# Rescheduling a fused attention and gated feed-forward kernel: eight heads per projection, background matmuls in every second slot, a pipelined prologue

## The chip, the cores and the metric

The kernel runs on one core of one Trainium2 chip. The metric is the device time of one execution in microseconds (us). Most executions of one kernel agree within 0.3% (the twelve of the old kernel lie between 1168.73 and 1172.42 us). Each run has a state; all comparisons here are between runs in the fast state, except where the text says otherwise. Engines are named as the profile names them: PE is TensorE (matmuls), PEld its weight loads, ACT is ScalarE, DVE is VectorE, POOL is GpSimd, SP is SyncE.

## The reference

The block has 2048 tokens of width 512, 32 heads of width 16 and a feed-forward width of 1792. All weights and inputs are bf16.

```python
def attention(x, wqkv, wo):                     # x: (1, 2048, 512)
    q, k, v = split_heads(x @ wqkv)             # 32 heads of 16
    p = softmax(q @ k.T * 16 ** -0.5)           # 2048 x 2048 for each head
    return merge_heads(p @ v) @ wo

def glu(x, w_gate, w_up, w_down):               # F = 1792
    return (sigmoid(x @ w_gate) * (x @ w_up)) @ w_down

h  = x + attention(layernorm(x), wqkv, wo)
h2 = h + glu(layernorm(h), w_gate, w_up, w_down)
```

The softmax needs 32 x 2048 x 2048 exponentials.

## The kernel before

The kernel has three parts: a prologue (layer norm, transposes, the first projections), a main loop over tiles of scores, and a tail (output projection and feed-forward of the last quarter of the queries).

One turn of the main loop handles three units of 128 keys x 512 queries of one head. I call a turn a **slot**. There are 683 of them, in four query chunks of about 171 slots. In a slot PE computes the next tile of scores (three row-tiled matmuls, K = 32), ACT computes one exponential over 1536 columns, and PE multiplies older exponentials with V (column-tiled matmuls, M = 17). Everything else (projections of later heads, output projection, feed-forward of the chunk before) is **background**: generators that advance by one step in every slot.

```python
    pss_next = scores(groups[0])
    for n, group in enumerate(groups):            # one slot
        pss = pss_next
        if n + 1 < len(groups):
            pss_next = scores(groups[n + 1])      # two score buffers
        pt = ptp.tile([P, GU, QC], BF16, name="pt")
        nc.scalar.activation(out=pt[:, 0:w, :], in_=pss[:, 0:w, :], func=ACT.Exp,
                             scale=DH ** -0.5)
        av(GU if len(avq) <= 2 * GU else 2 * GU)  # three value matmuls, or six
        ...
        step()                                    # one background step, mostly 4 matmuls
```

A projection handles four heads at a time, each padded with zeros from 16 to 32 rows so that it lands where the row-tiled scores want it. So half of each projection matmul multiplies zeros:

```python
    def proj_T(ps, w_pad, g, c, a=0, b=DC):
        for d in range(a, b):
            nc.tensor.matmul(ps[:], lhsT=w_pad[:, d, 4 * g:4 * g + 4, :].rearrange("p h r -> p (h r)"),
                             rhs=xnT[:, d, c * QC:(c + 1) * QC],
                             start=(d == 0), stop=(d == DC - 1))

    def prep_q(qc, g):                            # a background generator
        ps = pm_tile()                            # the only bank for the background
        proj_T(ps, wq_pad, g, qc)
        yield
        sq = q_evac(ps, qc, g)
        yield
        yield
        ps = pm_tile()
        q_shift_mm(ps, sq)                        # norms, for a bound on the scores
        yield
        q_shift(ps, qc, g)
```

The prologue does one chunk after the other, with all 16 tiles of V:

```python
    for c in range(NQC):
        chunk_ln(c)                  # statistics, normalise, transpose
        ...                          # padded weights, K of the first heads, Q of the first chunk
        for i in range(TQ):
            v_tile(bank0(), c * TQ + i, True)
    ...
    k4 = kmax_red(pk, 0)             # maxima, moved between partitions by four DMAs
```

## Time and profile before

The median is 1170.74 us. The profiled run is 1168.8 us long. First, the page's share of each engine, two rows of its table in 40 slices of the span (a digit is tenths busy; PEclk is the clock granted to PE; the clock records of this trace hold 1.0, printed as 9 and called full clock here, and 0.5, called half clock), and the chain that ended last:

```profile
PE 947.9 (81%) x5408; PEld 287.7 (25%) x5408; DVE 264.8 (23%) x526; ACT 981.0 (84%) x774; POOL 86.1 (7%) x82
...
ACT  2359889899987997999987997899988998999911
...
PEclk9778999776577998756678999765678998555589
...
ACT pt L471 37%; PE pm L147 6%; PE pss L403 6%; PE acc L431 5%; PE pm L352 4%; PE pss L502 2%; DVE hT L347 2%; PE pm L309 2%; PE b L201 2%; PE pm L336 1%; ACT th L340 1%; DVE xn L116 1%; DVE KT L156 1%; PE pm L344 1%; PE pss L511 1%
```

PE and ACT look equally busy, but matmul records overlap (at 448.46 us below, tiles of scores are recorded as 0.39 us long, and the value matmuls start 0.33 after them), so "81%" says little. The groups view (line, engine, operation, out<-in, count | busy us, mean ns | idle before it, and what ended that) says who waits for whom:

```profile
L471 ACT ACTIVATE pt<-pss 128x1536 bf16<-128x1536 f32 (+1 forms) x683 | 942.3, 1561 | 83.3 <-PE pss L403 61.0
L403 PE MATMUL pss<-qt,KT 32*128 32x512 bf16 x2048 | 337.2, 482 | 131.2 <-ACT pt L471 121.6
L147 PE MATMUL pm<-xnT,wq_pad 128*128 128x512 bf16 x124 | 50.4, 553 | 0.5 <-DVE sh L195 0.2
```

PE waits 121.6 us for ACT in front of the scores, so PE is not the bound on the whole; yet ACT waits 61.0 us for scores, so PE comes late at times. The padded Q projections take 553 ns in the mean, against 398 for the down projection (same shape), a first sign that they run at half clock (four of them hold PE for 1.82 us at half clock in this trace and for 0.96 at full). The mean of 1561 ns is not what one exponential costs: a record can start while the one before still runs (683 records of 1561 ns are 1066 us, but ACT was busy with them for 942.3). The ends of 520 of the 682 pairs of neighbouring exponentials lie 1.34 to 1.36 us apart, with a median of 1.344. So 683 of them need 918 us. A tanh between them (42 of them) is counted here with 0.44 us. The traces say 0.49: the intervals with a tanh in them are 1.834 us long in the median. What an interval has beyond 1.344 and 0.44 I call **loss**; it is worked out from the ends of the exponentials in the trace. So every loss below is about 2.1 us too high (42 x 0.05). The span then divides as follows.

| part of the span | us |
|---|---|
| until the first exponential starts | 73.7 |
| 683 exponentials x 1.344 | 918 |
| 42 tanh x 0.44 | 18.5 |
| loss: ACT late because PE was late | 100.1 |
| after the last exponential ends | 58.4 |

Where does the loss arise? The timeline (start us, duration, engine, line, what, count, and in brackets the idle time before it and what ended it) of a stretch at full clock, where a background step stands in each slot; weight loads are left out:

```profile
448.46 0.39 PE L403 MATMUL pss<-qt,KT 32*128 32x512 bf16 x3
448.79 0.39 PE L431 MATMUL acc<-pt,Vaug 128*17 128x512 bf16 x3
448.96 1.45 ACT L471 ACTIVATE pt<-pss 128x1536 bf16<-128x1536 f32 x1 [0.19 <-PE pss L403]
449.11 1.04 PE L352 MATMUL pm<-wd,hT 128*128 128x512 bf16 x4
450.08 0.39 PE L403 MATMUL pss<-qt,KT 32*128 32x512 bf16 x3
450.40 0.39 PE L431 MATMUL acc<-pt,Vaug 128*17 128x512 bf16 x3
450.57 1.45 ACT L471 ACTIVATE pt<-pss 128x1536 bf16<-128x1536 f32 x1 [0.16 <-PE pss L403]
```

From one tile of scores to the next PE needs 0.33 + 0.32 + 0.97 = 1.62 us, more than 1.344, so ACT idles 0.16 to 0.19 us before each exponential. A single full slot should be absorbed, since there are two score buffers (my reasoning); neighbouring full slots are not. Elsewhere a background step arrives at half clock:

```profile
532.24 0.61 PE L403 MATMUL pss<-qt,KT 32*128 32x512 bf16 x3 [0.20 <-ACT pt L471]
532.78 0.60 PE L431 MATMUL acc<-pt,Vaug 128*17 128x512 bf16 x3
533.58 0.61 PE L403 MATMUL pss<-qt,KT 32*128 32x512 bf16 x3 [0.20 <-ACT pt L471]
534.12 0.60 PE L431 MATMUL acc<-pt,Vaug 128*17 128x512 bf16 x1
534.65 1.79 PE L147 MATMUL pm<-xnT,wq_pad 128*128 128x512 bf16 x4
...
537.18 4.14 ACT L471 ACTIVATE pt<-pss 128x1536 bf16<-128x1536 f32 x3 [0.96 <-PE acc L431]
```

Slots without background work keep up at half clock (0.54 + 0.54 us < 1.344). But four full matmuls now take about 1.7 us, and ACT waits 0.96 us at once.

The background has one PSUM bank, and when the next background matmul has to wait until another engine has emptied the bank or made its operand, the scores that the program puts behind it on PE wait too.

The longest, 2.9 us, stand behind a finished group: DVE first works through four operations on the finished values (2.1 us) and only then empties the bank.

### The profile page before, as it was taken

The numbers are of one execution on the slowest core, as the hardware profiler recorded it, in microseconds if no ns is written. First come the engines' busy times: TensorE is split into PE (matmuls) and PEld (weight loads), VectorE is DVE, ScalarE is ACT, GpSimd is POOL, SyncE is SP. The second block draws the span as 40 slices with busy tenths as digits, with TensorE's granted clock in tenths as the row PEclk, the third lists the DMA queues.
The fourth block names the chain that finished last, engine by engine and source line by source line (L and its number), as shares of the span: only waits on it lengthen the run. The fifth ranks groups of instructions, "written<-read, shape, count | busy, mean of one in ns | idle before, by whom it ended". The sixth has DMA issues, their size and how long they took to land.

```text
span 1168.8 us, 13212 instructions
## 1 busy us (share of the span) xinstructions
PE 947.9 (81%) x5408; PEld 287.7 (25%) x5408; DVE 264.8 (23%) x526; ACT 981.0 (84%) x774; POOL 86.1 (7%) x82
## 2 busy tenths in 40 slices
PE   3668787878887988788887898788888988888878
PEld 1212222222222322222222232222222322222233
DVE  5423323311123211211123212211124211000063
ACT  2359889899987997999987997899988998999911
POOL 6022222200000000100000000100000000000000
PEclk9778999776577998756678999765678998555589
DMA  5000000050000000000000000000000001000000
GB/s 144 1 1 1 1 1 1 1 190 1 1 19 1 1 1 19 2 1 1 1 19 1 1 1 19 1 1 1 1 19 1 1 1 37 1 1 1 1 1 19
DMA packets 11741, 14.87 MB, mean 13 GB/s; under 512 B 928, under 2 KB 10528, under 8 KB 11680
## 3 DMA queue, kind: packets, MB, share of 16 engines
q1 hardware_dynamic: 9904, 11.93, 3.1%
q10 hardware_dynamic: 1584, 1.57, 0.4%
q0 software_dynamic: 192, 0.52, 0.3%
q8 instruction: 42, 0.69, 0.2%
q14 instruction: 19, 0.16, 0.0%
HBM read 11.80 MB, written 2.10 MB: 12 GB/s over the span
## 4 chain that ended last, share of the span: by engine, by line
ACT 39%; PE 33%; issue 15%; DVE 10%; DMA 1%; POOL 0%; SPq 0%; ACTq 0%; DVEq 0%; POOLq 0%
ACT pt L471 37%; PE pm L147 6%; PE pss L403 6%; PE acc L431 5%; PE pm L352 4%; PE pss L502 2%; DVE hT L347 2%; PE pm L309 2%; PE b L201 2%; PE pm L336 1%; ACT th L340 1%; DVE xn L116 1%; DVE KT L156 1%; PE pm L344 1%; PE pss L511 1%
## 5 line engine op out<-in xcount | busy, mean ns | idle before, releaser
L471 ACT ACTIVATE pt<-pss 128x1536 bf16<-128x1536 f32 (+1 forms) x683 | 942.3, 1561 | 83.3 <-PE pss L403 61.0
L403 PE MATMUL pss<-qt,KT 32*128 32x512 bf16 x2048 | 337.2, 482 | 131.2 <-ACT pt L471 121.6
L431 PE MATMUL acc<-pt,Vaug 128*17 128x512 bf16 x2048 | 340.2, 482 | 1.5 <-DVE xs L412 1.0
L403 PEld LDWEIGHTS <-KT 32*128 32x128 bf16 x2048 | 107.3, 94 | 410.4 <-issue 397.9
L431 PEld LDWEIGHTS <-Vaug 128*17 128x17 bf16 x2048 | 66.3, 89 | 222.9 <-issue 222.8
L412 DVE STREAM_TRANSPOSE xs<-acc 128x512 f32<-128x512 f32 x32 | 22.9, 717 | 430.5 <-PE acc L431 430.0
L161 POOL TENSOR_TENSOR sq<-qt 128x512 bf16<-128x512 bf16 x32 | 33.3, 1040 | 678.3 <-DVE qt L187 667.2
L347 DVE SCALAR_TENSOR_TENSOR hT<-th,pm 128x512 bf16<-128x512 f32 x42 | 28.8, 685 | 139.0 <-ACT pt L471 105.1
L336 PE MATMUL pm<-hnT,wg 128*128 128x512 bf16 x168 | 46.1, 399 | 10.8 <-DVE hT L347 10.8
L352 PE MATMUL pm<-wd,hT 128*128 128x512 bf16 x168 | 47.0, 398 | 9.4 <-DVE ob L362 8.6
L147 PE MATMUL pm<-xnT,wq_pad 128*128 128x512 bf16 x124 | 50.4, 553 | 0.5 <-DVE sh L195 0.2
L344 PE MATMUL pm<-hnT,wu 128*128 128x512 bf16 x168 | 44.1, 386 | 0.0
L340 ACT ACTIVATE th<-pm 128x512 f32<-128x512 f32 x42 | 32.9, 784 | 9.4 <-PE pm L336 9.4
L161 POOL TENSOR_TENSOR sq<-KT 128x512 bf16<-128x512 bf16 x32 | 33.3, 1040 | 99.7 <-DVE KT L156 57.6
L195 DVE TENSOR_SCALAR sh<-pm,kmax 4x512 bf16<-4x512 f32 x31 | 22.9, 738 | 67.3 <-PE acc L431 34.0
L505 ACT ACTIVATE th<-pss 128x512 f32<-128x512 f32 x14 | 8.4, 598 | 35.1 <-PE pss L502 35.1
L147 PE MATMUL pm<-xnT,wk_pad 128*128 128x512 bf16 x112 | 32.4, 416 | 6.2 <-DVE KT L156 6.2
L156 DVE TENSOR_SCALAR KT<-pm,e 128x512 bf16<-128x512 f32 x28 | 21.0, 750 | 38.3 <-PE pm L147 38.3
L309 PE MATMUL pm<-wo_pad,ot 128*128 128x512 bf16 x96 | 25.8, 393 | 4.3 <-DVE h L314 3.4
L122 PE MATMUL b<-ident_bf,xn 128*128 128x128 bf16 x64 | 7.2, 253 | 25.4 <-DVE xn L116 25.4
L187 DVE CAST qt<-pm 128x512 bf16<-128x512 f32 x31 | 20.8, 671 | 24.4 <-PE pm L147 24.4
L336 PEld LDWEIGHTS <-wg 128*128 128x128 bf16 x168 | 15.3, 99 | 32.0 <-issue 22.9
(84 smaller groups left out, 403.3 us busy)
## 6 DMA issues: line engine op xcount, KB each, us to landing
xb<-in_A_x_dram SPq DMA_DIRECT2D x4, 512.0 KB
xr<-in_A_x_dram SPq DMA_DIRECT2D x4, 512.0 KB
out_dram<-ob SPq DMA_DIRECT2D x16, 128.0 KB
wg<-in_B_w_gate_dram SPq DMA_DIRECT2D x1, 1792.0 KB
wu<-in_B_w_up_dram SPq DMA_DIRECT2D x1, 1792.0 KB
wd<-in_B_w_down_dram SPq DMA_DIRECT2D x1, 1792.0 KB
wk_raw<-in_A_wqkv_dram ACTq DMA_DIRECT2D x1, 512.0 KB
wv_sb<-in_A_wqkv_dram ACTq DMA_DIRECT2D x1, 512.0 KB
```

The costliest lines, as they stand in the source:

```text
L147: nc.tensor.matmul(ps[:], lhsT=w_pad[:, d, 4 * g:4 * g + 4, :].rearrange("p h r -> p (h r)"), rhs=xnT[:, d, c * QC:(c + 1) * QC], start=(d ...
L156: nc.vector.tensor_scalar(out=dst, in0=ps[:], scalar1=e16[:, 0:1], scalar2=None, op0=ALU.add)
L161: nc.gpsimd.tensor_tensor(out=sq[:], in0=src, in1=src, op=ALU.mult)
L309: nc.tensor.matmul(ps[:], lhsT=OT[qc, g][:, i * P:(i + 1) * P], rhs=wo_pad[:, g, :], start=(g == 0), stop=(g == NG - 1))
L336: nc.tensor.matmul(ps[:], lhsT=wg[:, d, f * P:(f + 1) * P], rhs=hnT[:, d, :], start=(d == 0), stop=(d == DC - 1))
L340: nc.scalar.activation(out=th[:], in_=ps[:], func=ACT.Tanh, scale=0.5)
L344: nc.tensor.matmul(ps[:], lhsT=wu[:, d, f * P:(f + 1) * P], rhs=hnT[:, d, :], start=(d == 0), stop=(d == DC - 1))
L347: nc.vector.scalar_tensor_tensor(out=hT[:, f, :], in0=th[:], scalar=1.0, in1=ps[:], op0=ALU.add, op1=ALU.mult)
L352: nc.tensor.matmul(ps[:], lhsT=hT[:, f, i * P:(i + 1) * P], rhs=wd[:, f, :], start=(f == 0), stop=(f == FC - 1))
L403: nc.tensor.matmul(pss[:, ui, :], lhsT=KT[g][32 * j:32 * j + 32, kt * P:(kt + 1) * P], rhs=QT[qc, g][32 * j:32 * j + 32, :], start=True, s ...
L431: nc.tensor.matmul(state["acc"][32 * j:32 * j + VW, :], lhsT=Vaug[:, kt, 4 * g + j, :], rhs=pt[:, ui, :], start=(kt == 0), stop=(kt == NT ...
L471: nc.scalar.activation(out=pt[:, 0:w, :], in_=pss[:, 0:w, :], func=ACT.Exp, scale=DH ** -0.5)
```

## The change

The change has four intents: fewer background matmuls (eight unpadded heads per projection, spread to their rows by small DMAs afterwards); no two overloaded slots side by side (value matmuls in even slots, up to four background matmuls in odd ones); a pipelined prologue with half of V moved out of it; and a tail whose output projection starts before the last heads are done. The diff has 966 lines; its core is:

```diff
-    def proj_T(ps, w_pad, g, c, a=0, b=DC):           # 4 padded heads
-            nc.tensor.matmul(ps[:], lhsT=w_pad[:, d, 4 * g:4 * g + 4, :]..., rhs=xnT[...])
+    def proj8(ps, w_sb, p, c, a=0, b=DC):             # 8 heads
+            nc.tensor.matmul(ps, lhsT=w_sb[:, d, p * P:(p + 1) * P], rhs=xnT[c][:, d, :], ...)
+    def spread(dst_pair, src, cols):                  # rows of a head to their place
+        for a in range(2):
+            for j in range(4):
+                eng = nc.sync if a == 0 else nc.gpsimd
+                eng.dma_start(out=dst_pair[a][32 * j:32 * j + DH, cols], in_=src[r:r + DH, :])
 ...                                                   # prologue
-    for c in range(NQC):
-        chunk_ln(c)
+    for c in range(NQC):
+        if c + 1 < NQC:
+            c_stats(c + 1)                            # next chunk's statistics first
+        c_trans(c, xns)
+        if c:
+            c_kmax(c - 1)                             # maxima by chunk, no DMA
+        if c + 1 < NQC:
+            xns = c_apply(c + 1)                      # normalise on DVE and ACT
+        c_proj(c)                                     # V only for t < NV0 = 8
 ...                                                   # main loop
-        av(GU if len(avq) <= 2 * GU else 2 * GU)
-        step()
+        if n % 2 == 0:
+            av(8)
+            run_bg(0)                                 # evacuations only
+        else:
+            run_bg(4)                                 # at most four matmuls
 ...                                                   # tail: warm-up matmuls
+    for k in range(16):
+        nc.tensor.matmul(junk, lhsT=wg[:, k % DC, 0:P], rhs=xnT[1][:, k % DC, :], ...)
```

## The prediction

> **What bounds it now.** ScalarE. The groups view has 683 exponentials (1536 columns each); the timeline shows back-to-back ones 1.344 us apart, so 918 us. [...] The 1169 us divide so:
> - 73.7 to the first exponential (timeline);
> - 918 of exponentials;
> - 18.5 for 42 tanh between them (0.44 each);
> - about 100 in which ScalarE waits for scores;
> - 58.4 after the last exponential.
>
> Slots without background matmuls lose nothing, even at half clock (scores 0.54 + values 0.54 < 1.344). The 100 us arise where four full 128x512 matmuls stand in one exponential's slot. Each switch between row-tiled scores, column-tiled values and full matmuls costs about 0.1 us ([...]the timeline agrees: six value matmuls 0.54 us, three 0.32). Full clock: 0.32 + 0.32 + 0.97 = 1.61 against 1.344, up to 0.27 lost. Half clock: 2.9, 1.5 lost. By slot, about half of the loss falls at half clock.
>
> **What the change does.**
> 1. Eight heads instead of four zero-padded ones per projection: background matmuls fall from 943 (266 slots) to 767 (210), by the instruction order, though 8 of 16 V tiles move from the prologue into the background.
> 2. Values and background alternate: mostly six values in one slot, four background matmuls in the next. A pair of slots needs 2x0.32 + 0.54 + 0.97 = 2.15 us at full clock against 2.69 for two exponentials: no loss. At half clock 0.54x2 + 0.97 + 1.82 = 3.9: about 1.2 lost.
> 3. Prologue pipelined: next chunk's statistics first, normalisation on two engines, maxima per chunk, no 2.6 us DMA round trip for them, no padded weights.
> 4. Cost: 16-partition DMAs spread K and Q; squares move to VectorE. Both have several slots of slack.
> 5. Tail: half the output projection, partly before the last group; warm-up matmuls.
>
> **Sum.** Before, clock windows with 58% or more streaming matmul time mostly stayed at full clock; those under 46% fell to half. The new pairs give about 64% (before, in the gate stage, 67%), so background stretches should stay warm and lose only at cold starts: about 22 x 1.2 = 26, plus 9 for evacuations queued behind a finished group: 35 instead of 100. First exponential near 50 instead of 73.7 (VectorE needs about 7 a chunk instead of 12.5; 7 from the last K projection to scores instead of 17). Tail 56.
> 50 + 918 + 18.5 + 35 + 56 = 1077, plus 1 to 2 from span to time: **1078 us, 8% faster; 8 in 10: 1052 to 1108.** Chances: faster by over 2% 0.97, within 2% 0.02, slower 0.01.
>
> **What the profile should show.** ScalarE's share up from 84% to about 90%; 683 exponentials, still 1.344 apart; their idle time behind scores far below 83 us; PE busy lower; remaining losses at half-clock slots with four background matmuls; first exponential near 50, 56 from the last to the end; in the chain of waits, the projections' 6% mostly gone.
>
> **What would make it wrong.** The granted clock: with less matmul work per time it may fall to half inside feed-forward stretches[...]. Spread K or Q arriving late. A finished group (2.1 us on VectorE) blocking the single background bank. GpSimd's clearing of K and Q tiles delaying the start (in the old trace a 3.8 us clear held one VectorE operation for 3.96).

1344 ns for an exponential is read from the trace. The 0.1 us for a switch is an estimate from the old trace: three value matmuls side by side hold PE for 0.32 us and six, in two rounds, for 0.54 at full clock, so a round is 0.22 and 0.10 is left over, which I put down to the switch; no run isolates it. The durations at half clock are from the same trace: 0.54 for three score matmuls, 0.96 for six value matmuls, 1.82 for four full ones. The clock windows with their 58% and 46% were read from the old trace's clock records. The 64% and 67% of streaming time are estimates (eight rounds of 0.22 us in the 2.69 us of a pair of slots are 65%). The 22 cold starts, the 7 us of DVE for a chunk and the 7 from the last K projection to scores are my estimates. The "2.6 us DMA round trip" is the time of four DMA issues on SP (66.30 to 68.91 us of the old trace); DVE waited 3.82 us for the data.

## More of the kernel before

From the waits view (who waited for whom: us in total, times, longest), three of the rows:

```profile
PE pm L336 <- DVE hT L347: 10.8, 14, 2.9
PE pm L352 <- DVE ob L362: 8.6, 3, 2.9
PE pm L122 <- DVE xn L116: 8.0, 3, 2.7
```

Within the exponentials such waits add up to 46.7 us.

The 2.7 us ones stand behind the standard deviations and the normalisation on DVE.

## The result, and the profile after

The changed kernel takes 1061.47 us (median of 8 runs, 1059.89 to 1063.67), against 1170.74 before. The ratio is 0.9069, with a 95% interval of 0.9059 to 0.9079. Ratios here are the mean time of one kernel's fast runs over the mean of the other's fast runs of the same rounds, so they are not quite the ratio of the medians. The result lies inside the predicted range, 16.5 us below the predicted point.

The page after, the same lines as before:

```profile
PE 828.5 (78%) x5212; PEld 229.6 (22%) x5212; DVE 232.3 (22%) x485; ACT 972.6 (92%) x777; POOL 82.2 (8%) x155
...
ACT  4699999999999999999999999999999999999721
...
PEclk9899865555579999965579999965579989955599
...
ACT pt L611 58%; PE pss L532 3%; PE pss L422 2%; ACT th L445 2%; PE acc L583 2%; PE pm L123 2%; PE pm L422 2%; PE pss L432 1%; DVE st L111 1%; DVE xs L548 1%; PE b L123 0%; PE b L161 0%; PE pm L161 0%; DVE KT L99 0%; DVE h L381 0%
...
L611 ACT ACTIVATE pt<-pss 128x1536 bf16<-128x1536 f32 (+1 forms) x683 | 932.2, 1667 | 19.8 <-PE pss L532 14.5
```

ACT is busy in nine tenths or more of nearly every slice between prologue and tail, and the exponentials' share of the chain rose from 37 to 58%. Note the mean of one exponential: 1667 ns, *more* than the 1561 before. It is the trap named above; the ends of 608 of 682 neighbours now lie 1.34 to 1.36 us apart, and the median is still 1.344. The idle time before them fell from 83.3 to 19.8 us. The waits of PE in front of background matmuls fell from 46.7 to 13.2 us; the largest row of them is now

```profile
PE pm L422 <- DVE hT L427: 5.5, 4, 1.9
```

Two slots of a feed-forward stretch at full clock:

```profile
346.82 0.39 PE L532 MATMUL pss<-QT,KT 32*128 32x512 bf16 x3 [0.41 <-ACT pt L611]
347.15 1.04 PE L422 MATMUL pm<-xnT,wg 128*128 128x512 bf16 x4
348.17 0.39 PE L532 MATMUL pss<-QT,KT 32*128 32x512 bf16 x3
348.49 0.60 PE L583 MATMUL acc<-pt,Vaug 128*17 128x512 bf16 x6
349.07 0.89 ACT L445 ACTIVATE th<-pm 128x512 f32<-128x512 f32 x1
349.51 0.39 PE L532 MATMUL pss<-QT,KT 32*128 32x512 bf16 x3 [0.42 <-ACT pt L611]
```

Now it is PE that waits for ACT (0.41 and 0.42 us). And the same kind of place as the one shown at half clock before, a query projection after a stretch without background:

```profile
464.34 0.61 PE L532 MATMUL pss<-QT,KT 32*128 32x512 bf16 x3 [0.20 <-ACT pt L611]
464.89 1.89 PE L123 MATMUL pm<-xnT,wq_sb 128*128 128x512 bf16 x4
...
467.94 5.48 ACT L611 ACTIVATE pt<-pss 128x1536 bf16<-128x1536 f32 x4 [0.96 <-PE acc L583]
```

This cost is still there, 0.96 us of ACT. There are fewer such places (the clock returned to full 34 times before, 16 times now). The parts of the span:

| part | before | predicted | after |
|---|---|---|---|
| to the first exponential | 73.7 | 50 | 43.8 |
| exponentials and tanh | 936.5 | 936.5 | 936.5 |
| loss | 100.1 | 35 | 22.1 |
| after the last exponential | 58.4 | 56 | 59.4 |

So about 78 us come from the loss, 30 from the prologue, and the tail gives 1 back.

### The profile page after: what moved, and what is told of

The parts are those of the page before. It is cut to its first block, busy times and chain, and to the rows that moved or that the text cites. A ratio compares the mean times of both kernels' runs of the same rounds, so it can differ in the third digit from the quotient of the medians.

```text
span 1061.8 us, 13184 instructions
## 1 busy us (share of the span) xinstructions
PE 828.5 (78%) x5212; PEld 229.6 (22%) x5212; DVE 232.3 (22%) x485; ACT 972.6 (92%) x777; POOL 82.2 (8%) x155
## 4 chain that ended last, share of the span: by engine, by line
ACT 60%; issue 20%; PE 14%; DVE 4%; DMA 1%; POOL 0%; ACTq 0%; SPq 0%; DVEq 0%; POOLq 0%
ACT pt L611 58%; PE pss L532 3%; PE pss L422 2%; ACT th L445 2%; PE acc L583 2%; PE pm L123 2%; PE pm L422 2%; PE pss L432 1%; DVE st L111 1%; DVE xs L548 1%; PE b L123 0%; PE b L161 0%; PE pm L161 0%; DVE KT L99 0%; DVE h L381 0%
## 5 line engine op out<-in xcount | busy, mean ns | idle before, releaser
L611 ACT ACTIVATE pt<-pss 128x1536 bf16<-128x1536 f32 (+1 forms) x683 | 932.2, 1667 | 19.8 <-PE pss L532 14.5
L532 PE MATMUL pss<-QT,KT 32*128 32x512 bf16 x2048 | 333.1, 475 | 191.5 <-ACT pt L611 185.7
L583 PE MATMUL acc<-pt,Vaug 128*17 128x512 bf16 x2048 | 263.3, 483 | 0.4 <-ACT pt L611 0.3
L131 POOL DMA_DIRECT2D QT<-qd x64 | 31.0, 487 | 628.0 <-DVE qd L136 609.2
L583 PEld LDWEIGHTS <-Vaug 128*17 128x17 bf16 x2048 | 36.5, 89 | 110.2 <-issue 109.8
L422 PE MATMUL pm<-xnT,wg 128*128 128x512 bf16 x168 | 47.7, 410 | 5.5 <-DVE hT L427 5.5
L422 PE MATMUL pm<-xnT,wu 128*128 128x512 bf16 x168 | 43.9, 384 | 3.4
L131 POOL DMA_DIRECT2D KT<-kd x64 | 30.9, 490 | 55.0 <-ACT kd L224 26.2
L422 PEld LDWEIGHTS <-wu 128*128 128x128 bf16 x224 | 21.2, 97 | 29.5 <-issue 10.5
L422 PEld LDWEIGHTS <-wg 128*128 128x128 bf16 x224 | 19.4, 100 | 33.8 <-issue 18.6
L432 PEld LDWEIGHTS <-hT 128*128 128x128 bf16 x224 | 18.0, 97 | 26.0 <-issue 10.9
L123 PE MATMUL pm<-xnT,wq_sb 128*128 128x512 bf16 x60 | 23.2, 529 | 0.0
L154 DVE TENSOR_SCALAR sh<-pm,kcol 8x512 bf16<-8x512 f32 x15 | 11.1, 738 | 15.2 <-PE pm L336 15.2
```

Source lines behind the costliest of these rows:

```text
L123: nc.tensor.matmul(ps, lhsT=w_sb[:, d, p * P:(p + 1) * P], rhs=xnT[c][:, d, :], start=(d == 0), stop=(d == DC - 1))
L131: eng.dma_start(out=dst_pair[a][32 * j:32 * j + DH, cols], in_=src[r:r + DH, :])
L154: nc.vector.tensor_scalar(out=sh[:], in0=ps[0:8, :], scalar1=-0.505, scalar2=kcol[p][:, 0:1], op0=ALU.mult, op1=ALU.add)
L422: nc.tensor.matmul(ps, lhsT=w[:, d, f * P:(f + 1) * P], rhs=hnT[:, d, :], start=(d == 0), stop=(d == DC - 1))
L432: nc.tensor.matmul(ps, lhsT=hT[:, f, i * P:(i + 1) * P], rhs=wd[:, f, :], start=(f == 0), stop=(f == FC - 1))
L532: nc.tensor.matmul(pss[:, ui, :], lhsT=KT[g][32 * j:32 * j + 32, kt * P:(kt + 1) * P], rhs=QT[g][32 * j:32 * j + 32, :], start=True, stop= ...
```

## The experiments

Everything below is measured against the old kernel in the same rounds. "First" is the start of the first exponential, "half" the time within the exponentials at half clock, "returns" how often the clock came back to full there. These four columns come from the profiled run of each kernel.

| kernel | median us | ratio (95%) | first | loss | half | returns |
|---|---|---|---|---|---|---|
| before | 1170.74 | 1 | 73.7 | 100.1 | 486 | 34 |
| after | 1061.47 | 0.907 (0.906-0.908) | 43.8 | 22.1 | 425 | 16 |
| e1, background in every slot | 1119.46 | 0.956 (0.955-0.958) | 43.9 | 77.9 | 620 | 23 |
| e2, values in every slot | 1061.86 | 0.907 (0.906-0.909) | 44.1 | 20.3 | 396 | 14 |
| e3, both in every slot | 1110.33 | 0.949 (0.947-0.951) | 42.9 | 72.5 | 591 | 21 |
| e4, 144 matmuls more | 1066.51 | 0.911 (0.910-0.913) | 44.1 | 26.5 | 340 | 18 |
| e5, kept warm | 1054.74 | 0.901 (0.899-0.903) | 43.7 | 11.2 | 51 | 10 |
| e6, all of V first | 1070.60 | 0.915 (0.913-0.916) | 49.8 | 26.0 | 463 | 20 |
| e7, statistics not ahead | 1071.51 | 0.915 (0.914-0.917) | 53.5 | 22.0 | 435 | 20 |
| e8, tail without warm-up | 1063.13 | 0.908 (0.907-0.910) | 43.0 | 20.5 | 423 | 19 |
| e9, old kernel, spaced | 1145.37 | 0.979 (0.978-0.981) | 73.5 | 76.4 | 360 | 23 |
| e10, old kernel, kept warm | 1169.74 | 0.999 (0.997-1.001) | | | | |
| e11, kept warmer | 1054.71 | 0.902 (0.900-0.903) | 43.4 | 15.3 | 53 | 15 |
| e12, e10 again, one run | 1167.58 | none | 71.4 | 99.4 | 167 | 29 |

All gave correct results.

### Which part of the schedule matters: e1, e2, e3

The theory (A) says that overloaded neighbouring slots make the loss, so spacing the background removes it. Rivals: the smaller number of background matmuls (B), and batching six to eight value matmuls, with fewer switches of PE's tiling mode (C). Three kernels put one or both of the new placements back, with the new kernel's instructions:

```diff
         if n % 2 == 0:
             av(8)
-            run_bg(0)
-        else:
-            run_bg(4)
+        run_bg(4)                                  # e1: background in every slot

-        if n % 2 == 0: ... else: ...
+        av(4)
+        run_bg(4 if n % 2 else 0)                  # e2: values in every slot

-        if n % 2 == 0: ... else: ...
+        av(4)
+        run_bg(4)                                  # e3: both
```

(e1 and e3 also pause one slot after a tanh is issued, as the old kernel does; otherwise the next matmuls would wait for the tanh in the only background bank.)

Expected of e1:

> The changed kernel, with background matmuls allowed in every slot instead of every second one (a slot's pause after a tanh, as in the old kernel), value matmuls still six or eight in every second slot. Same instructions, other places. Theory A (spacing: the old loss came from overloaded neighbouring slots): the loss of ScalarE returns in part, from 22 us to 45 to 75 us, so 1085 to 1115 us. Rival B (fewer background matmuls made the gain): within 8 us of 1061. Rival C (batching the value matmuls made it): within 10 us of 1061, since the batching stays.

Expected of e2 (the 2.25 us are an estimate, 4 x 0.32 + 0.97 from the old trace; at half clock 4 x 0.54 + 1.82 = 3.98 against 2 x 0.54 + 0.96 + 1.82 = 3.86):

> The changed kernel, with value matmuls in every slot (at most four, mostly three), background matmuls still in every second slot only. A: 2.25 us of work per pair of slots at full clock is still below 2.69, so no loss where the clock is full; at half clock the pair is about 0.1 us longer: 1060 to 1068 us. B: the same, 1061. C: most of the old loss returns, 1090 us or more.

Expected of e3:

> The changed kernel, with both in every slot: the old kernel's placement with the new kernel's fewer matmuls. A: loss of 50 to 85 us in place of 22: 1090 to 1125 us, and more than the run with only the background in every slot. B: within 8 us of 1061. C: 1090 or more, and clearly more than the run with only the background in every slot.

Measured: e2 is the new kernel to within its interval, so batching the value matmuls is worth nothing and C falls. e3 loses 72.5 us in place of 22.1, 49 us of time: inside A's range, and B falls as the sole cause. e1 is 58 us slower, 4 us beyond the range I gave. I had expected e3 to lose more than e1; it was the other way round by 9 us. By the instruction order, e1 has slots with six or eight value matmuls *and* four background ones; with the durations of the traces that is 0.32 + 0.54 + 0.97 = 1.83 us in place of 1.61. So batching without spacing does harm.

### The same test on the old kernel: e9

```diff
+    def step_spaced(odd):
+        if odd:
+            while bg and not step1():        # run until a step has issued matmuls
+                pass
+        elif bg and flag.get(id(bg[0])) == 0:
+            step1()                          # an evacuation only
 ...
-        step()
+        if n < len(groups) // NQC:           # chunk 1: as before
+            step()
+        else:
+            step_spaced(n % 2)
```

The first chunk is left alone, since there the old kernel's 210 background matmuls, against 122 in the new one, have deadlines every 21 slots.

> The old kernel, where in query chunks 2 to 4 the background matmuls run in every second slot only (evacuations that need no matmul may run in the other); nothing else is changed, and its 943 padded background matmuls stay. A: of the 100 us lost, some 70 fall in those chunks, and 40 to 55 of them go: 1115 to 1131 us. B: 1165 to 1175 us. C: the same as B, since value matmuls stay in every slot.

Measured: 1145.4 us. Spacing alone takes 25 us off the old kernel (ratio 0.9775 to 0.9805: clear of noise, though by the record's mark of 2% the verdict is "unclear"), so it works there too, but my 40 to 55 us were a miss. With the value matmuls in every slot in all four kernels, the loss in chunks 2 to 4, where e9 differs, forms a square:

| loss in chunks 2 to 4, us | background in every slot | in every second slot |
|---|---|---|
| old kernel (four padded heads) | 75.0 (before) | 51.3 (e9) |
| new kernel (eight heads, V partly in background of chunk 1) | 50.6 (e3) | 14.5 (e2) |

Spacing takes off 24 us in the old kernel and 36 in the new one; the rest of the new main loop takes off 24 or 37, and together they take off 60. Neither is the cause alone. But the rows of the square differ in more than packing: the new kernel also gives every evacuation a step of its own, which runs in the slot before the next matmuls, and makes the squares on DVE in place of POOL. So I looked for the waits of PE for another engine in front of background matmuls. A slot counts as beside a wait when at least 0.3 us of one lie between 1.34 us before the end of the exponential before and its own end; "near half clock" is defined under e10 below.

| us | before | e9 | e1 | e3 | e2 | after |
|---|---|---|---|---|---|---|
| waits of PE in front of background matmuls | 46.7 | 51.0 | 50.9 | 33.3 | 8.5 | 13.2 |
| loss beside such a wait | 44.7 | 54.0 | 38.4 | 37.2 | 4.5 | 7.1 |
| other loss near half clock | 40.2 | 19.7 | 27.6 | 20.2 | 13.4 | 12.6 |
| other loss, at full clock | 15.1 | 2.8 | 11.8 | 15.2 | 2.4 | 2.4 |

(Most of the second row is near half clock too, 34.2 of the 44.7 before, since the clock fell while PE waited, as at 826.6 us of the new trace, from 1.0 to 0.5 within a wait of 1.85 us; these slots can't be divided between the two causes.) Three things follow. Neighbouring overloaded slots at full clock, the cause that theory A began with, are in the last row: at most 15 of the old 100 us, and spacing does remove them. The largest part of the old loss lies beside waits for evacuations and squares. And these explain e9: its own edit moved the matmul on the squares one slot closer to them, PE waited 16.7 us for POOL's squares in place of 8.4, and in chunks 2 to 4 the loss beside those waits grew from 2.3 to 17.6 us. Beside all such waits e9 lost 41.7 of its 51.3 us there and e2 3.8 of 14.5. So the 37 us between e9 and e2 lie almost wholly beside such waits, and fewer matmuls or query projections can explain little of them; of the 24 us between the old kernel and e3, 6 do.

In the new kernel spacing and the separate evacuations work together: with the background in every slot (e1) the waits come back, 50.9 us. No run changes the evacuations alone, or gives the background a second bank; this rival to spacing and packing stays untested.

### Does the number of matmuls matter by itself: e4

```diff
         proj8(ps, wq_sb, p, qc, 2, 4)
+        for _ in range(1 if qc else 0):      # the same projection once more
+            yield 2
+            proj8(ps, wq_sb, p, qc, 0, 2)
+            yield 2
+            proj8(ps, wq_sb, p, qc, 2, 4)
 ...
             wo_mm(ps, qc, i, 2, 4)
+            for _ in range(2):               # the same output projection twice more
+                yield 2
+                wo_mm(ps, qc, i, 0, 2)
+                yield 2
+                wo_mm(ps, qc, i, 2, 4)
```

> The changed kernel with 144 useless background matmuls more (query projections of chunks 2 to 4 done twice, output projections of chunks 1 to 3 three times; the result is unchanged): 911 in place of 767, near the 943 of the old kernel, in 36 more of the every-second slots, each next to slots that already have some, so no new cold starts. A (loss comes from overloaded neighbouring slots and from cold starts): loss 20 to 28 us, 1059 to 1068 us. B (the count of background matmuls sets the loss: 78 us for 176 matmuls between the two kernels, 0.44 each): about 63 us more, 1125.

Measured: 1066.5 us, 5 us more, where B said 63. With 911 background matmuls in place of 767, spaced, the loss rose from 22.1 to 26.5 us. In this schedule, added matmuls are nearly free while they stay in slots that have room and prolong stretches that already run; in the old placement it was not tried.

### What is left of the loss: e5, e11

```diff
             run_bg(4)
+            if st["mm_at"] < n and (not bg or bg[0][2] in ("wait", "go")):
+                ps = pm_tile()
+                for k in range(DC):          # result is never read
+                    nc.tensor.matmul(ps, lhsT=wq_sb[:, k, 0:P], rhs=xnT[1][:, k, :],
+                                     start=True, stop=True)
```

> The changed kernel with four useless matmuls in every second slot that has no background work (131 slots). D (the 22 us that are left are cold starts of the clock): half-clock time within the exponentials falls from 425 us to below 60, loss from 22 to 3 to 9 us: 1043 to 1050 us. E (what is left comes from waits for evacuations, transfers and tanh): loss stays at 18 to 25 us, 1058 to 1065.

The profile, busy time between the first exponential and the last (us, then PE, PEld, DVE, ACT, POOL busy, then the granted clock, DMA share, GB/s), of the new kernel:

```profile
43.80:1002.50 958.70, 755.19 (x4857) 196.71 (x4855) 176.57 (x353) 942.61 (x725) 65.17 (x120) 0.78 0.05 14
```

and the same part with the useless matmuls:

```profile
43.70:991.40 947.70, 765.87 (x5385) 250.73 (x5383) 175.58 (x353) 939.87 (x725) 64.98 (x120) 0.97 0.05 14
```

The clock in this part rose from 0.78 to 0.97, and the part shrank by 11 us. This is the fastest kernel, 1054.7 us. But the profiled run was the fastest of its four (1051.8; the others 1054.5 to 1056.3), so the 11.2 us of loss flatter it; the median gives 6.7 us of gain. I had expected 1043 to 1050. What the useless matmuls removed is thus a third (by the medians) to a half (by the profiles) of what was left, not nearly all. Of the 11.2 us that remained in the profile, 9.3 still lie near half clock (counted as under e10 below), and 4.9 beside waits of PE as defined under e9.

The clock still fell (ten returns to full in e5's trace), by my reading around the background's transposes, which are short: in the new kernel's trace four of them hold PE for 0.54 us at half clock. e11 adds six half-width useless matmuls behind each:

```diff
-            pt = transpose4(pm_tile(), hn)
+            pm = pm_tile()
+            pt = transpose4(pm, hn)
+            for k in range(6):
+                nc.tensor.matmul(pm[:, 256:512], lhsT=wq_sb[:, k % DC, 0:P],
+                                 rhs=xnT[1][:, k % DC, 0:256], start=True, stop=True)
```

> The kernel with useless matmuls in empty every-second slots (1054.7 us, loss 11 in its profile, of which 9 near half clock), with six more half-width ones behind each background transpose tile, where the clock still fell. If those drops make most of what is left: half-clock time from 51 to below 30 us, loss 5 to 9: 1047 to 1053 us. If not, 1053 to 1057.

Measured: 1054.7 us, the same as e5, half-clock time did not fall (53 us), and the clock returned 15 times in place of 10. This try failed, and what makes up the last 11 to 15 us stays open in part.

### Is it half clock, or the cold start: e10, e12

Counting an exponential as near half clock when at least 0.5 us of half clock lies between 2 us before the end of the one before it and its own end, 74.5 of the old kernel's 100 us of loss lie there (after: 19.7 of 22.1). Does half clock then explain three quarters of the old loss? e10 keeps the old kernel warm wherever its background queue is empty:

```diff
+        if not bg and n % 2:
+            ps = pm_tile()
+            for k in range(DC):
+                nc.tensor.matmul(ps[:], lhsT=wq_pad[:, k, 0:4, :].rearrange("p h r -> p (h r)"),
+                                 rhs=xnT[:, k, 0:QC], start=True, stop=True)
         step()
```

> The old kernel, with four useless matmuls in every second slot in which its background queue is empty; its placement, padding and prologue stay. Of its 100 us of loss, 74 fall in exponentials with half clock near them. If the clock alone explains them: half-clock time within the exponentials falls from 486 us to 100 to 250, and loss from 100 to 55 to 80 us: 1125 to 1150. If dense placement would lose as much at full clock: 1160 to 1172.

Measured: its three fast runs took 1167.6 to 1170.5 us, no gain (inside the second range), at a granted clock of 0.92 where the old kernel has 0.78. The kernel ran once more for a profile:

> The old kernel with useless matmuls in its empty slots once more, for a profile in the fast state: its fast runs took as long as the old kernel (1167.6 to 1170.5) at a mean clock of 0.92 in place of 0.78, and its profile fell in the slow state. If dense placement loses as much at full clock, the loss is 95 to 105 us with 60 or more of it in slots away from half clock (25.6 in the old kernel). If the useless matmuls cost by themselves, the loss sits in slots next to them, in stretches that lost nothing before (the second half of each chunk).

This single run (state unknown, as always for one run; its time and clock are those of the three fast ones) settles it. Half-clock time within the exponentials fell from 486 to 167 us, and the loss stayed: 99.4 us, 69.7 of it near half clock, 29.7 elsewhere. Neither of the two outcomes that I had written down fits. The timeline shows what happened at a query projection; L479 are the useless matmuls:

```profile
280.33 0.61 PE L403 MATMUL pss<-qt,KT 32*128 32x512 bf16 x3 [0.20 <-ACT pt L471]
280.88 0.60 PE L431 MATMUL acc<-pt,Vaug 128*17 128x512 bf16 x3
281.41 1.89 PE L479 MATMUL pm<-xnT,wq_pad 128*128 128x512 bf16 x4
...
283.94 6.82 ACT L471 ACTIVATE pt<-pss 128x1536 bf16<-128x1536 f32 x5 [0.97 <-PE pss L403]
```

The projection itself now ran warm, at 272.9 us. But while the rest of its generator waited, the queue was not empty, no useless matmul was issued for some slots, the clock fell, and the *first useless matmuls* paid the cold start: ACT waits 0.97 us, as much as a cold projection cost. The cold start has only moved. Over the whole trace, a query projection came first in the 3.8 us before a return of the clock 19 times before and 5 times in e12, the useless matmuls 9 times. And the useless matmuls leave the waits of PE alone: 45.6 of e12's 99.4 us lie beside one, 44.7 before. So half-clock time without background cost nothing (in the old kernel 243 slots with 0.5 us of loss in sum), and a start from half clock cost about a microsecond in the places shown, whoever started.

The clock returned to full 29 times in e12 and 34 times before, but 16 times in the new kernel and 10 times in e5. The count alone does not set the loss, though: e3 and e7 have 21 and 20 returns, and 72.5 and 22.0 us of loss. Per return, the loss near half clock is 2.2 us before, 2.4 in e12 and 2.3 in e3, but 1.2 in the new kernel and 1.0 in e7. So the new schedule made a return cheaper as well as rarer; what the other microsecond was made of (full slots side by side while cold, or the waits) no run separates.

### The prologue: e6, e7

```diff
-    NV0 = 8
+    NV0 = 16                                  # e6: all V tiles in the prologue

-        if c + 1 < NQC:
-            c_stats(c + 1)
         c_trans(c, xns)
 ...
         c_proj(c)
+        if c + 1 < NQC:                       # e7: statistics behind the projection
+            c_stats(c + 1)
+            xns = c_apply(c + 1)
```

> The changed kernel with a chunk's statistics and normalisation issued after the chunk before it is projected, not ahead of its transposes. F (issuing ahead is what the prologue gains by): first exponential 8 to 16 us later: 1069 to 1078 us. G (the gain is from shared normalisation, unpadded weights and the shorter end; VectorE has the same work): 0 to 4 us later, 1061 to 1066.

Measured: the first exponential starts at 53.5 us, 9.7 later, and the time is 10 us longer: F. The four K projections start at 15.8, 25.7, 32.5 and 35.4 us in the new kernel, at 13.4, 24.9, 35.0 and 45.1 in e7, and at 18.7, 32.4, 45.0 and 56.6 in the old one.

> The changed kernel with all 16 V tiles in the prologue, as the old one had them, in place of 8. The prologue's matmul time grows by 32 matmuls of 0.22 to 0.43 us; VectorE sets the pace there, with 7 us a chunk, so part of it is hidden: first exponential 3 to 8 us later than 43.8, loss after it 1 to 3 us smaller: 1063 to 1068 us.

(The 0.22 to 0.43 us are an estimate for one round of 512 columns at full and at half clock: (0.97 - 0.10) / 4 and (1.82 - 0.10) / 4 from the old trace.)

Measured: the first exponential is 6.0 us later, as expected, but the loss grew by 4 us where I had said that it would shrink, and 1070.6 us is outside my range. The timeline of e6 shows why:

```profile
58.66 1.82 POOL L270 MEMSET KT<- 128x2048 bf16 x1
...
60.41 3.88 POOL L131 DMA_DIRECT2D KT<-kd  x8
63.88 0.69 DVE L136 CAST kd<-pm 128x512 bf16<-128x512 f32 x1 [5.90 <-DMA KT<-kd]
...
67.13 8.32 ACT L611 ACTIVATE pt<-pss 128x1536 bf16<-128x1536 f32 x6 [4.43 <-PE pss L532]
```

Half of the row-spreading DMAs are issued by POOL, behind its clearing of the K and Q tiles, which lasts until 60.4 us. The third staged K chunk needs a staging buffer whose DMA has not been issued yet, waits 5.9 us, holds the only background bank, and ACT loses 4.4 us. In the new kernel the eight V tiles fill just this time. So moving them is worth about 9 us in time: 6 in the prologue, and a good part of the rest in this queue.

### The tail: e8

```diff
-    junk = pm_tile()
-    for k in range(16): ...                   # warm-up
 ...
         pt = transpose4(hps[i], hn)
-        for k in range(3): ...                # warm-up between the transposes
```

> The changed kernel without the 28 useless matmuls of its tail (16 while VectorE works out the standard deviations, 3 after each of four transposed tiles). The tail took 59.4 us, 3.4 more than predicted; the feed-forward's first matmul comes 19.5 us after the last exponential, 17.2 in the old kernel. H (the 12 matmuls between the transposes hold up the tail): first matmul at 17.5 to 18.5, but cold, the first pair of projections about 1.5 us slower: tail 58.5 to 59.5, time within 2 us of 1061. I (the warm-up is worth more than it costs): tail 60 to 62.

Measured: 1063.1 us, 1.7 more by the medians, with intervals of the ratios that overlap (0.907 to 0.910 against 0.906 to 0.908). In the traces, the first feed-forward matmul comes 18.6 us after the last exponential in place of 19.5, but the first gate and up projections then take 3.4 us in place of 1.7; the tail is 60.1 us long in place of 59.4. The tail lies in I's range, the time in H's, and the first matmul just outside H's; the warm-up about pays for itself, and neither is clearly right. Why did the halved output projection not shorten the tail? In both kernels a chain on DVE decides: the standard deviations are ready 13.4 us after the last exponential before and 13.0 after. From there to the first feed-forward matmul the old kernel needs 3.8 us, the new one 6.5 and e8 5.5: normalising and transposing tile by tile with two buffers takes longer than doing all four at once with four. That last reading is argued from the traces; no run separates it.

## Why the prediction was right, point by point

- **The bound.** ACT bounds the kernel at 1.344 us per exponential. Right: unchanged count and spacing, share of ACT 92% (predicted about 90).
- **Where the 100 us arise.** Only in part right. The prediction put them down to four full matmuls in one slot, at full and at half clock. By the table under e9, 44.7 us lay beside waits of PE for the background bank or its operand, which the prediction had only among its risks ("a finished group (2.1 us on VectorE) blocking the single background bank"). In the old kernel PE waited behind a finished group in 11 places, for 25.6 us; 36.6 us of loss stand there, and 11 of the 34 returns of the clock follow.
- **Spacing removes the loss at full clock.** Right where PE does not wait. Away from half clock and from such waits the loss fell from 15.1 to 2.4 us (2.1 of which is the tanh counted too short), and it is 11.8 in e1, 15.2 in e3 and 2.8 in e9.
- **Loss that stays.** The term was 35 us, it measured 22.1. The step that was mis-sized: "about 22 x 1.2 = 26". The clock returned 16 times, not 22. The "plus 9 for evacuations queued behind a finished group" was near: the interval in which a group finishes has no loss, but in 8 places PE then waits 1.1 to 1.9 us for the bank, and the slots there lose 8.6 us together. That leaves 13.5 us for the other 14 returns (2.1 of it the tanh counted too short), about 1.0 each at most.
- **The clock stays full in background stretches.** Right for the most part: the feed-forward that runs in chunks 2 and 3 had full clock for 133 us without a break; in chunk 4 it fell twice, each time after PE had waited behind a finished group. Streaming time is an estimate: 512 columns count with 0.22 us at full clock and 0.43 at half (worked out as above), and three tiles side by side once. All clock records of the two traces but the last of each, which the end cuts off, are multiples of 3.41 us long; a window is 3.41 us here. Counted so, windows of the new trace that stayed at full clock had a median of 59% of it, those that fell 35%. So the lower of the two figures read from the old trace held (33 of its 35 falling windows and all 16 of the new one are below 46%); the upper one was no limit, since 38% of the windows that stayed in the new trace lie under it.
- **"By slot, about half of the loss falls at half clock."** Too simple. By the wider count it was three quarters, and e12 showed that half-clock time is not what costs (486 us of it before and 167 in e12, at 100.1 and 99.4 us of loss); the clock returned to full nearly as often, 29 times against 34.
- **The prologue.** The term was 50 us, it measured 43.8. "VectorE needs about 7 a chunk" was near (the K projections are 6.5 us apart on average, but 9.9, 6.8 and 2.9 one by one; the last chunk has no statistics behind it); "7 from the last K projection to scores" was 7.7, or 8.4 to the first exponential. With 3 x 7 and 7 the predicted 50 leaves 22 for the first K projection, which started at 15.8: the start was over-estimated. Of the 30 us won, e7 shows 9.7 for issuing the statistics ahead and e6 shows 6.0 for V; the other 14 (unpadded weights, the shorter end, the shared normalisation) are not separated by runs.
- **The clears on POOL.** Named as a risk. In the old trace a clear of 3.8 us held one DVE operation for 3.96 us (the 16 operations of its kind have a median of 0.41); why it was held no run shows. In the new kernel the clears instead hold up POOL's own DMA queue, which e6 made visible.
- **The tail.** The term was 56 us, it measured 59.4: the shorter output projection is off the tail's critical path, and the transposes became slower.

## What to carry to other kernels

When a bounding engine is fed through two buffers, place side work so that no two neighbouring turns are overloaded; side work with room around it was nearly free here, even when there was more of it (e4: 144 more matmuls, 5 us). Look as closely for places where the feeding engine itself waits in order for an evacuation, and give the evacuation a turn of its own before the next matmuls. Half clock between such stretches cost nothing here (0.5 us in 243 slots); what cost was a stretch that started cold (about 1 us of ACT in the three starts shown), and keeping the clock up helped only where it took away starts (e5: 10 in place of 16, 6.7 us; e12: 29 in place of 34, no gain). And judge an engine by the distance between the ends of its instructions, because the mean of the records can grow while the engine gets faster (1561 to 1667 ns here, with the ends still 1.344 us apart).

## What the traces show of the clock and the records

- Row- and column-tiled matmuls alone did not bring full clock: in the old kernel only these ran from 990.2 to 1110.4 us, and the granted clock was 0.5 throughout. They streamed for 0.85 of each 1.344 us (63%, an estimate: two rounds of 512 columns at 0.43 us each). In the old kernel, windows before a return to full clock had a median of 88% of streaming time; windows that fell from full clock had 46% or less in 33 of 35 cases.
- A cold start cost about 1 us of ACT in the three starts shown (0.96 at 537.18 us before, 0.97 at 283.94 in e12, 0.96 at 467.94 after), and 1.2 us of loss near half clock per return in the new kernel against 2.2 in the old one, while half clock between starts cost nothing (243 slots of the old kernel at half clock without background had 0.5 us of loss in sum).
- The slow run of e10, on one core, took 1228.7 us at a mean granted clock of 0.712; its three fast runs took 1167.6 to 1170.5 at 0.916 to 0.921.
- A change of the tiling mode cost about 0.1 us, an estimate: three concurrent 512-column tiles hold PE for 0.32 us, six for 0.54, so a round of 512 columns is 0.22 and 0.10 is left for the switch.
- The mean duration of back-to-back activations in a profile rose while their spacing stayed: the mean of one exponential's record went from 1561 to 1667 ns, while the median distance of their ends stayed 1.344 us. In e5 the mean was 1838 ns.
